# Two heads' scores as row tiles, two query tiles to a group, and a batch's scatters placed later in GpSimd's queue

## The chip, the cores and the metric

The kernel runs on one core of a Trainium2 chip. The metric is device microseconds (us) of one execution; less is better. PE is TensorE, DVE is VectorE, ACT is ScalarE, POOL is GpSimd, and SP is the engine whose queue issues the plain DMAs.

## The reference

Three stages run one after the other: causal windowed attention with a few global keys, then a mixture of experts in which each token goes to its best expert, then a second one with a fixed capacity for each expert.

```python
batch, n_heads, seq, head_dim = (4, 8, 768, 64)
n_global, n_local = (8, 96)
...
scores = scale * np.matmul(q, k.transpose(0, 1, 3, 2))
...
scores = scores + bias[None, :, :, :]
scores = np.where(keep, scores, -1000000000.0)
scores = scores - np.max(scores, axis=-1, keepdims=True)
a = np.exp(scores)
a = a / (np.sum(a, axis=-1, keepdims=True) + 1e-09)
return np.matmul(a, v).astype(np.float32)
...
x = np.ascontiguousarray(attn_out.transpose(0, 2, 1, 3)).reshape(B * S, H * D)
x = _moe_ref(x=x, **moe_kwargs)
return _moe2_ref(x=x, **moe2_kwargs)
```

The change lies in the attention stage and in the hand-over of its rows to the first experts, whose inputs are 3072 tokens of 512 numbers.

## The kernel before

The 4 batches and 8 heads make 16 pairs of heads, of which each is one step n = 4 b + hp of a loop. A head has 64 dimensions, so a pair's transposed queries and keys fill the 128 partitions. The 768 queries are six query tiles of 128. For query tile 0 a score tile has 128 columns (its own keys); for the others it has 232: 8 global keys, 96 before the tile and its own 128.

One step consists of these parts, by the lines of the profile:

- `prep` of the pair after this one: 12 transposes on PE (L402) bring keys (`kn`) and queries (`qn`) into PSUM tiles `tp`. DVE copies the keys into `kx` (L411, L414). ACT copies the queries into `qd` (L406), head 0 into partitions 0 to 63 of its first half, head 1 into partitions 64 to 127 of its second half; the other partitions of both halves were set to zero once. So a score matmul contracts over all 128 partitions, and the zeros cancel the other head's keys. POOL makes `va` and the global columns of `kx` by three copies (L417, L418, L420).
- `pair`: for each query tile two score matmuls on PE, one for each head (L444, into a PSUM tile `sc`, of which there are two, one bank each); DVE adds the bias and takes the minimum (L456); ACT takes the exponential (L458). PE transposes the probabilities into `pt` (L470), ACT copies them (`pts`, L472), and PE multiplies them with `vn` and `va` into `up` (L482), head 0 in output columns 0 to 63 and head 1 in 64 to 127 of the array.
- The results `ut` are copied out by DVE (L485), transposed on PE (L500) and scaled into the row tile `xr` (L501). After a batch's fourth pair `route` works out each token's place, and six indirect DMAs on POOL (L86, 128 rows each) scatter `xr` to `xs`. Experts read `xs` later: early loads `xa` of expert 0's first 240 rows (L604, on SP) are transposed on PE at L151 while attention is still running.

Every float32 matmul on two operands is recorded as two MATMULs with a LDWEIGHTS each. The order of an engine's instructions is made by a scheduler when the kernel is built; only SP's queue stands as written. PE, ACT, DVE and POOL each work through theirs in order, and an instruction that waits holds back all behind it. After attention, PE's order is written out by hand and is the same in both kernels. Scatters of batches 0 to 2 are issued from the loop by

```python
if n >= 6:
    while rows:
        rows.pop(0)()
```

Of the kernel before, what the change touches and what calls it, by code (L numbers as in the profile page):

```python
# [21 lines left out]
ROW = 516  # L22
# [7 lines left out]
def attention_moe_moe_kernel(  # L30
# [127 lines left out]
    def layer1(wa, xt, n, hs, cut=False, tags=("hp",)):  # L158

        xh, xl = xt  # L160
        for f in range(KF):
            if len(hs) == f:
                hs.append((m2.tile([128, SL], F32R, name=f"hh{f}"), m2.tile([128, SL], F32R, name=f"hl{f}")))
            hh, hl = hs[f]
            c = slice(f * 128, (f + 1) * 128)
            m = n // 2 if cut and f == 0 else n
            t_ = tags[f % len(tags)]
            for c0 in range(0, n, m):
                t = slice(c0, c0 + m)
                hp_ = pool_of[t_].tile([128, 512], F32, name="hp", tag=t_, bufs=1 if t_ == "gp" else None)  # L170
# [85 lines left out]
    with ExitStack() as actx:  # L256
# [114 lines left out]
        qds = []  # L371
        for i in range(2):
            qd = ac.tile([128, 2, S], F32, name=f"qd{i}")
            nc.gpsimd.memset(qd[0:64, 1], 0.0)
            nc.gpsimd.memset(qd[64:128, 0], 0.0)
            qds.append(qd)
        z = qds[0][64:128, 0, 0:ROW]
# [9 lines left out]

        def prep(b, hp, loads, first=False):
            qn, kn, vn = loads
            va = None  # L390
            qd = qds[hp % 2]
# [4 lines left out]
            if True:  # L396
                for (src, is_q), (g0, g1) in order:
# [6 lines left out]
                    if is_q:  # L404
                        for h in range(2):
                            nc.scalar.activation(qd[64 * h:64 * h + 64, h, c0:c0 + n],  # L406
                                                 tp[64 * h:64 * h + 64, :n], AF.Copy, scale=-0.125)
                    else:
                        t0, t1 = c0 // 128, (c0 + n) // 128
                        tpv = tp[:, :n].rearrange("p (t j) -> p t j", j=128)  # L410
                        nc.vector.tensor_copy(kx[:, t0:t1, k0:], tpv)  # L411
                        if not dense:
                            t2 = min(t1 + 1, NT)
                            nc.vector.tensor_copy(kx[:, t0 + 1:t2, 32:128], tpv[:, :t2 - t0 - 1, 32:128])  # L414
            if not dense:
                va = a2.tile([128, NT - 1, 2, D], F32, name="va")
                nc.gpsimd.tensor_copy(va, vn[:, :NT - 1])  # L417
                nc.gpsimd.tensor_copy(va[0:32], vgs[hp % 2][:, None].to_broadcast([32, NT - 1, 2, D]))  # L418
                if n_global:
                    nc.gpsimd.tensor_copy(kx[:, 1:, G0:32],  # L420
                                          kx[:, 0:1, 128:160 - G0].to_broadcast([128, NT - 1, 32 - G0]))
            return qd, kx, vn, va

        def pair(b, hp, ready, ut, sums, tiles=range(NT)):
            qd, kx, vn, va = ready
            upb = {}
            for t in tiles:
                if dense:
                    cols = [(0, 512), (512, S - 512)]
                    W, off, HW = S, 0, 1024  # L430
                elif t == 0:
                    W, off, HW = 128, 128, 256
                else:
                    W, off, HW = 256, G0, 256
                sc = ps.tile([128, 2, HW], F32, name="sc")
                p = a3.tile([128, 2, W], F32, name="p", tag="p") if dense else pbufs[t % 3]
                for h in range(2):
                    lhs = qd[:, h, 128 * t:128 * t + 128]
                    if dense:
                        for c0, n in cols:  # L440
                            nc.tensor.matmul(sc[:, h, c0:c0 + n], lhs,
                                             kx[:, c0 // 128:(c0 + n) // 128], start=True, stop=True)
                    else:
                        nc.tensor.matmul(sc[:, h, off:], lhs, kx[:, t, off:], start=True, stop=True)  # L444
# [60 lines left out]
        def route(b, ut, rec, xr, parts, tags=("tp", "tp")):  # L505
# [57 lines left out]
            return lambda: [scatter("xs", xs, si[:, t:t + 1], xr[:, T0 + t]) for t in range(nt)]  # L563
# [5 lines left out]
        batch, rows = {}, []  # L569
        todo = None  # L570
        for n in range(B * NP):
# [17 lines left out]
            if n >= 6:  # L589
                while rows:  # L590
                    rows.pop(0)()
# [17 lines left out]
            def todo(parts=(0, 3), tags=("tp", "tp"), steps="fn", b=b, hp=hp, ut=ut, uts=uts, sums=sums, rec=rec, xr=xr):  # L609
                if "f" in steps:  # L610
                    factors(hp, sums, rec, parts)
                    if hp == NP - 1:
                        rows.append(route(b, uts, rec, xr, parts, tags))
# [3 lines left out]
            if n < B * NP - 2:  # L617
                pair(b, hp, cur, ut, sums)
# [4 lines left out]
            else:  # L623
# [11 lines left out]
                rows.pop()()  # L635
# [11 lines left out]
        rows.pop()()  # L647

        counted = pick_order("tp")
        if EB:  # L650
# [12 lines left out]
            l1 = layer1(pre[0], xta, EA, hsa, tags=("sc",))  # L663
# [725 lines left out]
```

## Time and profile before

| | |
|---|---|
| median of 3 runs | 1009.27 us (1006.7 to 1011.89) |
| the profiled execution, its own time | 1016.74 us |
| its span in the trace, first to last instruction | 1015.0 us |
| PE busy | 951.0 us, 94% of the span |
| ACT busy | 425.0 us, 42% |
| DVE busy | 557.0 us, 55% |
| POOL busy | 298.5 us, 29% |
| granted TensorE clock, mean | 0.974 |

Attention fills about the first 250 us of the span. The shares are means over all stages. A busy PE counts the whole record of a matmul, from issue to a modelled end; records overlap, so the time that one more matmul costs is the distance between two starts, not the length of a record.

### The profile page before, as it was taken

Reading aid. Unit: us, or ns where it says so; the run is one execution under the profiler, and the core shown is the slowest. Engines: PE = TensorE matmul, PEld = TensorE weight load, DVE = VectorE, ACT = ScalarE, POOL = GpSimd, SP = SyncE. Lnnn points to the kernel's source line nnn. Section 1 sums busy time; section 2 is a strip of 40 time slices with the busy share of each in tenths; the row PEclk is TensorE's granted clock in tenths of the full one; section 3 lists DMA queues with packets and bytes.
Section 4 is the critical chain, followed back from the end, with each engine's and each line's share of the span. In section 5 each row is a group of like instructions: output and inputs, shape, how many; then the busy total and the mean of one; then the engine's idle time right before and its main releaser. Section 6 shows DMA issues by size and latency. Waiting matters only on the chain.

```text
span 1015.0 us, 17456 instructions
## 1 busy us (share of the span) xinstructions
PE 951.0 (94%) x6253; PEld 782.6 (77%) x6253; DVE 557.0 (55%) x1928; ACT 425.0 (42%) x939; POOL 298.5 (29%) x268
## 2 busy tenths in 40 slices
PE   8999889989996999999999979699999999999997
PEld 6877667767796999899897756487768677777996
DVE  6656566556332443423334344877878676785630
ACT  6886777856242433334224310133332323333531
POOL 3112333331235364464514861301020211102011
PEclk9999999999997999999999999889999999999999
DMA  7999654630355346534342311515243351615510
GB/s 156 212 200 211 165 144 123 136 120 3 118 175 178 126 143 206 149 136 136 125 146 83 111 44 40 207 53 187 94 146 128 102 187 42 219 65 176 169 59 31
DMA packets 124192, 133.24 MB, mean 131 GB/s; under 512 B 83445, under 2 KB 83585, under 8 KB 124097
## 3 DMA queue, kind: packets, MB, share of 16 engines
q1 hardware_dynamic: 114449, 105.96, 37.1%
q0 software_dynamic: 9648, 26.09, 7.8%
q8 instruction: 51, 0.84, 0.4%
q14 instruction: 44, 0.36, 0.1%
HBM read 103.77 MB, written 28.23 MB: 130 GB/s over the span
## 4 chain that ended last, share of the span: by engine, by line
PE 50%; issue 7%; DVE 7%; DMA 4%; POOL 2%; ACT 2%; POOLq 0%; SPq 0%; ACTq 0%; DVEq 0%
PE hp L175 22%; PE yp L207 13%; PE yp L191 7%; DMA raw<-in_moe_w_dram 3%; DVE wal L121 2%; PE hp L151 2%; ACT wah L119 1%; PE ip L1273 1%; POOL lg_dram L86 1%; PE cg L1125 1%; DVE wbl L121 1%; DVE geT L1114 1%; PE cp L1132 1%; PE hp L826 1%; PE hp L912 1%
## 5 line engine op out<-in xcount | busy, mean ns | idle before, releaser
L179 ACT ACTIVATE hh<-hp 128x384 fp32r<-128x384 f32 (+9 forms) x130 | 63.4, 491 | 200.3 <-PE hp L175 180.5
L180 DVE SCALAR_TENSOR_TENSOR hl<-hp,hh 128x384 fp32r<-128x384 f32 (+9 forms) x130 | 71.8, 555 | 117.9 <-ACT hh L179 113.6
L86 POOL DMA_INDIRECT out_dram<-yo,idx x24 | 25.8, 1074 | 265.6 <-ACT yo L1351 236.2
L458 ACT ACTIVATE pb<-pb,mn 128x232 f32<-128x232 f32 (+1 forms) x192 | 88.9, 465 | 18.6 <-DVE mn L456 18.1
L121 POOL TENSOR_TENSOR wbl<-raw,wbh 128x1024 fp32r<-128x1024 f32 x28 | 66.3, 2386 | 95.5 <-ACT wbh L119 55.5
L207 PE MATMUL yp<-wah,hh 128*128 128x512 f32 x224 | 93.0, 415 | 0.0
L444 PE MATMUL sc<-kx,qd 128*128 128x232 f32 (+1 forms) x384 | 90.4, 360 | 1.7 <-ACT qd L406 1.1
L207 PE MATMUL yp<-wah,hl 128*128 128x512 f32 x224 | 91.7, 410 | 0.0
L175 PE MATMUL hp<-xl,wah 128*128 128x240 f32 (+8 forms) x260 | 91.6, 352 | 0.0
L121 DVE TENSOR_TENSOR wal<-raw,wah 128x512 fp32r<-128x512 f32 (+1 forms) x78 | 67.4, 904 | 44.1 <-ACT wah L119 43.4
L175 PE MATMUL hp<-xh,wah 128*128 128x240 f32 (+8 forms) x260 | 90.7, 349 | 0.8 <-DVEq L835 0.6
L207 PE MATMUL yp<-wal,hh 128*128 128x512 f32 x224 | 91.0, 406 | 0.0
L119 ACT ACTIVATE wbh<-raw 128x1024 fp32r<-128x1024 f32 x60 | 62.3, 1057 | 68.2 <-DMA raw<-in_moe_w_dram 64.7
L175 PE MATMUL hp<-xh,wal 128*128 128x240 f32 (+8 forms) x260 | 90.5, 348 | 0.0
L175 PE MATMUL hp<-xh,wbh 128*128 128x384 f32 (+1 forms) x260 | 90.3, 347 | 0.0
L175 PE MATMUL hp<-xh,wbl 128*128 128x384 f32 (+1 forms) x260 | 89.9, 346 | 0.0
L175 PE MATMUL hp<-xl,wbh 128*128 128x384 f32 (+1 forms) x260 | 89.7, 345 | 0.0
L119 ACT ACTIVATE wah<-raw 128x1024 fp32r<-128x1024 f32 x68 | 68.5, 1052 | 43.1 <-DMA raw<-in_moe_w_dram 41.3
L456 DVE CUSTOM_DVE_ANT_0 pb<-sc,bias_w 128x232 f32<-128x232 f32 x160 | 56.9, 394 | 34.2 <-PE sc L444 18.0
L444 PEld LDWEIGHTS sc<-kx,qd 128*128 128x128 f32 x384 | 65.8, 199 | 9.6 <-issue 3.0
L121 POOL TENSOR_TENSOR wal<-raw,wah 128x1024 fp32r<-128x1024 f32 x22 | 58.2, 2657 | 43.2 <-ACT wah L119 26.6
L191 PE MATMUL yp<-hh,wbh 128*128 128x240 f32 (+5 forms) x192 | 65.2, 340 | 2.3 <-ACT yt L197 2.0
(303 smaller groups left out, 2145.4 us busy)
## 6 DMA issues: line engine op xcount, KB each, us to landing
raw<-in_moe_w_dram SPq DMA_DIRECT2D x128, 512.0 KB
xs_dram<-qd SPq DMA_DIRECT2D x8, 1032.0 KB
vn<-in_v_dram SPq DMA_DIRECT2D x32, 192.0 KB
kn<-in_k_dram SPq DMA_DIRECT2D x30, 192.0 KB
qn<-in_q_dram SPq DMA_DIRECT2D x30, 192.0 KB
rawg<-in_moe_w_dram SPq DMA_DIRECT2D x8, 512.0 KB
XB<-xs_dram SPq DMA_DIRECT2D x9, 241.9 KB
XB<-xs_dram SPq DMA_DIRECT2D x7, 258.0 KB
```

The costliest lines, as they stand in the source:

```text
L86: st = nc.gpsimd.indirect_dma_start(out=dst, out_offset=bass.IndirectOffsetOnAxis(ap=idx, axis=0), in_=src, in_offset=None)
L119: nc.scalar.activation(hi, raw, AF.Copy)
L121: lo_engine.tensor_tensor(lo[:, c], raw[:, c], hi[:, c], op=OP.subtract)
L151: tr = nc.tensor.transpose(tp[:, kk], rows[:, kk * 128:(kk + 1) * 128], ident[0:nt, 0:nt])
L175: nc.tensor.matmul(hp_[:, :m], a[:, c], b_[:, kk, t], start=(i == 0), stop=(i == 3 * KD - 1))
L179: nc.scalar.activation(hh[:, t], hp_[:, :m], AF.Relu)
L180: nc.vector.scalar_tensor_tensor(hl[:, t], hp_[:, :m], 0.0, hh[:, t], op0=OP.max, op1=OP.subtract)
L191: nc.tensor.matmul(yp, a[:, c], b_[:, :n], start=(f == 0 and i == 0), stop=(f == KF - 1 and i == 2))
L207: last_mm[0] = nc.tensor.matmul(yp, a[:, c], b_, start=(f == 0 and i == 0), stop=(f == KF - 1 and i == 2))
L444: nc.tensor.matmul(sc[:, h, off:], lhs, kx[:, t, off:], start=True, stop=True)
L456: nc.vector.tensor_tensor_reduce(p[:, h, off:], sc[:, h, off:], bt, 1.0, 3.0e38, OP.add, OP.min, mn)
L458: nc.scalar.activation(p[:, h, off:], p[:, h, off:], AF.Exp, bias=mn, scale=-1.0, accum_out=sums[:, t, hh:hh + 1])
```

## The change

It does these things:

- `qd` is one tile of 128 partitions (two buffers) without zero halves, filled by one ACT copy where there were two.
- A score matmul contracts over the 64 partitions of its head. Head 0 uses array rows 0 to 63 and head 1 rows 64 to 127; in the built program these matmuls have a tile size of 64 x 128, at row 0 and row 64.
- The scores of two query tiles are issued as one group of four matmuls into one PSUM tile of two banks, bank 0 for head 0 and bank 1 for head 1. There is one such tile, where there were two of one bank each.
- The scatters of a batch are held back by one step and are placed, one for each query tile, behind that tile's transposes, and behind POOL's copies for the next pair. This settles their place in the queue; they wait for nothing more at run time. For the last batch they stay where they were.
- The zeros that are written to `xs` come from a tile of their own.

```diff
-        z = qds[0][64:128, 0, 0:ROW]
+        z = ac.tile([64, ROW], F32, name="z")
+        nc.gpsimd.memset(z, 0.0)
...
+        last_copies = []
+
         def prep(b, hp, loads, first=False):
...
-            qd = qds[hp % 2]
+            qd = a2.tile([128, S], F32, name="qd")
...
                     if is_q:
-                        for h in range(2):
-                            nc.scalar.activation(qd[64 * h:64 * h + 64, h, c0:c0 + n],
-                                                 tp[64 * h:64 * h + 64, :n], AF.Copy, scale=-0.125)
+                        nc.scalar.activation(qd[:, c0:c0 + n], tp[:, :n], AF.Copy, scale=-0.125)
...
-                    else:
-                        nc.tensor.matmul(sc[:, h, off:], lhs, kx[:, t, off:], start=True, stop=True)
+                    W, off = (128, 128) if t == 0 else (256, G0)
+                    if i_ % 2 == 0:
+                        sc2 = ps.tile([128, 2, 2, 256], F32, name="sc", bufs=1)
+                        for k_, u in enumerate(tiles[i_:i_ + 2]):
+                            o = 128 if u == 0 else G0
+                            for h in range(2):
+                                hs_ = slice(64 * h, 64 * h + 64)
+                                nc.tensor.matmul(sc2[:, h, k_, o:], qd[hs_, 128 * u:128 * u + 128], kx[hs_, u, o:],
+                                                 start=True, stop=True)
+                    sc = sc2[:, :, i_ % 2]
+                    p = pbufs[t % 3]
...
-                            nc.tensor.transpose(pt[:, c, h], p[:, h, p0 + (c0 + c) * 128:p0 + (c0 + c + 1) * 128], ident)
+                            tr = nc.tensor.transpose(pt[:, c, h], p[:, h, p0 + (c0 + c) * 128:p0 + (c0 + c + 1) * 128], ident)
+                    if put:
+                        with tc.issue_after(tr.ins):
+                            put.pop(0)()
...
-            return lambda: [scatter("xs", xs, si[:, t:t + 1], xr[:, T0 + t]) for t in range(nt)]
+
+            def put(t):
+
+                st = scatter("xs", xs, si[:, t:t + 1], xr[:, T0 + t])
+                for c in last_copies:
+                    tc.add_manual_dep(st.ins, c.ins.name, mybir.DependencyInfo(
+                        mybir.DependencyClass.NoSync, mybir.DependencyReason.DATA), reason="order on GpSimd")
...
-            if n >= 6:
-                while rows:
-                    rows.pop(0)()
+            put = []
+            if 6 <= n < B * NP - 2:
+                put, late, rows = late, rows, []
...
-                pair(b, hp, cur, ut, sums)
+                pair(b, hp, cur, ut, sums, put=put)
+                for f in put:
+                    f()
```

How the built programs stand, at three places. The first is PE's queue in the middle of batch 0's fourth pair, from the scores of the pair's third query tile on (before: `sc_853`; after: `sc_813`). Before:

```order
L444 MATMUL sc_853<-kx_573,qd1_173 128x232 x2
L482 MATMUL up_685<-pts_731,va_422 64x128 x2
L482 MATMUL up_685<-pts_731,vn_388 64x128 x2
L470 MATMUL pt_821<-ident_71,pb1_166 128x128 x4
L444 MATMUL sc_874<-kx_573,qd1_173 128x232 x2
L500 MATMUL tp_784<-ident_71,ut_617 128x128 x3
L470 MATMUL pt_841<-ident_71,pb2_168 128x128 x4
L444 MATMUL sc_894<-kx_573,qd1_173 128x232 x2
```

PE's queue at the same place after the change (L445 is the score matmul, L474 the transposes, L489 the product with v, L507 the transposes of `ut`):

```order
L445 MATMUL sc_813<-kx_561,qd_560 128x232 x4
L489 MATMUL up_669<-pts_714,va_412 64x128 x2
L489 MATMUL up_669<-pts_714,vn_379 64x128 x2
L474 MATMUL pt_789<-ident_71,pb0_164 128x128
L507 MATMUL tp_766<-ident_71,ut_603 128x128 x3
L474 MATMUL pt_802<-ident_71,pb1_166 128x128 x4
L474 MATMUL pt_824<-ident_71,pb2_168 128x128
L507 MATMUL tp_771<-ident_71,ut_603 128x128 x3
L489 MATMUL up_788<-pts_792,vn_551 64x128 x2
L474 MATMUL pt_824<-ident_71,pb2_168 128x128 x3
L445 MATMUL sc_854<-kx_561,qd_560 128x232 x4
```

Two score matmuls for each tile became four for every two tiles, and they now stand next to full-array transposes with another tile size.

The second is POOL's queue around the scatters of batch 1. Before:

```order
L417 COPY va_1986<-vn_1952 128x640
L86 DMA xs_dram_66<-xr_917,si_1796 24576x516 x3
L418 COPY va_1986<-vg0_119 32x640
L86 DMA xs_dram_66<-xr_917,si_1796 24576x516 x3
L420 COPY kx_1961<-kx_1961 128x5x8
L121 TENSOR_TENSOR wal3_2309<-raw_2306,wah3_2308 128x1024
```

POOL's queue there after the change (L412, L413 and L415 are the three copies):

```order
L412 COPY va_1938<-vn_1905 128x640
L413 COPY va_1938<-vg0_119 32x640
L415 COPY kx_1915<-kx_1915 128x5x8
L86 DMA xs_dram_66<-xr_896,si_1758 24576x516 x6
L121 TENSOR_TENSOR wal3_2260<-raw_2257,wah3_2259 128x1024
```

The six scatters moved behind all three copies for pair 10, and still follow each other.

The third is POOL's queue around the scatters of batch 2, where the last two pairs of the loop are prepared. Before:

```order
L417 COPY va_2788<-vn_2754 128x640
L418 COPY va_2788<-vg0_119 32x640
L86 DMA xs_dram_66<-xr_1699,si_2592 24576x516 x6
L420 COPY kx_2763<-kx_2763 128x5x8
L417 COPY va_2969<-vn_2935 128x640
L418 COPY va_2969<-vg1_121 32x640
L420 COPY kx_2944<-kx_2944 128x5x8
```

POOL's queue there after the change:

```order
L412 COPY va_2724<-vn_2691 128x640
L413 COPY va_2724<-vg0_119 32x640
L415 COPY kx_2701<-kx_2701 128x5x8
L86 DMA xs_dram_66<-xr_1662,si_2538 24576x516 x6
L412 COPY va_2907<-vn_2874 128x640
L415 COPY kx_2884<-kx_2884 128x5x8
L413 COPY va_2907<-vg1_121 32x640
```

They moved behind `kx` of pair 14 and now stand between it and the copies for pair 15.

## Rows read from the trace of the kernel before

**Rows 1.** The page, part 1: busy us, share of the span, instructions.
```profile
PE 951.0 (94%) x6253; PEld 782.6 (77%) x6253; DVE 557.0 (55%) x1928; ACT 425.0 (42%) x939; POOL 298.5 (29%) x268
```

**Rows 2.** Stretches of attention: start:end, length, busy us and instructions, clock, DMA share, GB/s.
```profile
20.00:80.00 60.00, 60.00 (x486) 46.89 (x486) 37.72 (x170) 49.40 (x158) 6.86 (x13) 1.00 1.01 202
80.00:120.00 40.00, 37.10 (x295) 29.38 (x294) 23.06 (x102) 28.04 (x86) 13.23 (x16) 0.96 0.86 190
120.00:160.00 40.00, 36.34 (x295) 26.76 (x294) 24.78 (x103) 27.82 (x84) 16.91 (x16) 0.96 0.64 161
160.00:200.00 40.00, 40.00 (x310) 31.01 (x309) 24.72 (x113) 34.85 (x106) 9.91 (x11) 1.00 0.54 122
200.00:240.00 40.00, 36.02 (x282) 27.42 (x281) 24.75 (x119) 27.49 (x88) 12.73 (x14) 0.96 0.24 77
```

**Rows 3.** Groups by line, 0 to 400 us: busy, mean ns, idle before.
```profile
L444 PE MATMUL sc<-kx,qd 128*128 128x232 f32 x320 | 78.9, 371 | 1.0 <-DVE mn L456 0.6 <-ACT qd L406 0.3
L444 PE MATMUL sc<-kx,qd 128*128 128x128 f32 x64 | 13.0, 306 | 0.8 <-ACT qd L406 0.8
L444 PEld LDWEIGHTS sc<-kx,qd 128*128 128x128 f32 x384 | 65.8, 199 | 9.6 <-issue 3.0 <-DVE mn L456 2.7 <-ACT qd L406 2.0
L456 DVE CUSTOM_DVE_ANT_0 pb<-sc,bias_w 128x232 f32<-128x232 f32 x160 | 56.9, 394 | 34.2 <-PE sc L444 18.0 <-PE pt L470 8.8 <-ACT pb L458 5.6
L406 ACT ACTIVATE qd<-tp 64x256 f32<-64x256 f32 (+1 forms) x64 | 30.8, 482 | 9.0 <-PE tp L402 8.3
```

**Rows 4.** Timeline of PE, 228 to 252 us: start, length of the run, records.
```profile
232.55 0.95 PE L444 MATMUL sc<-kx,qd 128*128 128x232 f32 x4
233.33 0.49 PE L470 MATMUL pt<-ident,pb 128*128 128x128 f32 x3
...
237.51 0.39 PE L482 MATMUL up<-pts,vn 128*64 128x128 f32 x4
237.83 0.66 PE L470 MATMUL pt<-ident,pb 128*128 128x128 f32 x4
238.32 0.95 PE L444 MATMUL sc<-kx,qd 128*128 128x232 f32 x4
239.20 0.44 PE L482 MATMUL up<-pts,va 128*64 128x128 f32 x4
...
239.79 1.09 PE L470 MATMUL pt<-ident,pb 128*128 128x128 f32 x8
...
242.63 0.39 PE L482 MATMUL up<-pts,vn 128*64 128x128 f32 x4
242.84 0.39 PE L482 MATMUL up<-pts,va 128*64 128x128 f32 x4
```

**Rows 5.** Timeline of all engines in batch 1's scatters; in brackets idle time, releaser.
```profile
149.31 0.72 POOL L418 COPY va<-vg 32x640 f32<-32x640 f32 x1
150.20 0.99 POOL L86 DMA_INDIRECT xs_dram<-xr,si  x1 [0.17 <-issue]
151.49 0.96 POOL L86 DMA_INDIRECT xs_dram<-xr,si  x1 [0.30 <-issue]
152.32 0.56 DVE L485 COPY ut<-up 128x384 f32<-128x384 f32 x1 [3.78 <-remote]
152.44 0.60 ACT L472 ACTIVATE pts<-pt 128x512 f32<-128x512 f32 x1 [1.81 <-remote]
152.94 0.44 PE L482 MATMUL up<-pts,va 128*64 128x128 f32 x4 [2.49 <-issue]
```

**Rows 6.** Timeline: batch 2's first and last scatter, xa's loads, their first use.
```profile
207.97 1.01 POOL L86 DMA_INDIRECT xs_dram<-xr,si  x1 [2.21 <-DVE xr L558]
...
214.36 0.96 POOL L86 DMA_INDIRECT xs_dram<-xr,si  x1 [0.30 <-issue]
...
217.70 1.65 SPq L604 DMA_DIRECT2D xa<-xs_dram  x2
...
229.08 0.57 PE L151 MATMUL hp<-ident,xa 120*128 120x120 f32 x4
```

More of the change, by code (lines that the diff above doesn't have):

```diff
@@ L422, in prep, with pair @@
+                last_copies[:] = copies
             return qd, kx, vn, va
-        def pair(b, hp, ready, ut, sums, tiles=range(NT)):
+        def pair(b, hp, ready, ut, sums, tiles=range(NT), put=()):
             qd, kx, vn, va = ready
             upb = {}
-            for t in tiles:
+            tiles = list(tiles)
+            for i_, t in enumerate(tiles):
                 if dense:
                     cols = [(0, 512), (512, S - 512)]
-                    W, off, HW = S, 0, 1024
-                elif t == 0:
-                    W, off, HW = 128, 128, 256
-                else:
[L434 to L442, printed above, removed]
-                    else:
-                        nc.tensor.matmul(sc[:, h, off:], lhs, kx[:, t, off:], start=True, stop=True)
@@ new lines, in pair @@
+                    W, off = S, 0
+                    sc = ps.tile([128, 2, 1024], F32, name="sc")
+                    p = a3.tile([128, 2, W], F32, name="p", tag="p")
+                    for h in range(2):
+                        hs_ = slice(64 * h, 64 * h + 64)
+                        for c0, n in cols:
+                            nc.tensor.matmul(sc[:, h, c0:c0 + n], qd[hs_, 128 * t:128 * t + 128],
+                                             kx[hs_, c0 // 128:(c0 + n) // 128], start=True, stop=True)
+                else:
+                    W, off = (128, 128) if t == 0 else (256, G0)
[3 more added lines that the diff above has]
+                            o = 128 if u == 0 else G0
+                            for h in range(2):
+                                hs_ = slice(64 * h, 64 * h + 64)
+                                nc.tensor.matmul(sc2[:, h, k_, o:], qd[hs_, 128 * u:128 * u + 128], kx[hs_, u, o:],
+                                                 start=True, stop=True)
+                    sc = sc2[:, :, i_ % 2]
+                    p = pbufs[t % 3]
@@ L562, in route @@
             nc.vector.tensor_add(cum, cum, cs)
-            return lambda: [scatter("xs", xs, si[:, t:t + 1], xr[:, T0 + t]) for t in range(nt)]
+            def put(t):
[3 more added lines that the diff above has]
+                        mybir.DependencyClass.NoSync, mybir.DependencyReason.DATA), reason="order on GpSimd")
+            return [lambda t=t: put(t) for t in range(nt)]
         last_tr = [None]
@@ L568, in attention_moe_moe_kernel @@
             biases(range(2, H))
-        batch, rows = {}, []
+        batch, rows, late = {}, [], []
         todo = None
@@ L612, in todo @@
                     if hp == NP - 1:
-                        rows.append(route(b, uts, rec, xr, parts, tags))
+                        rows.extend(route(b, uts, rec, xr, parts, tags))
                 if "n" in steps:
@@ L634, in attention_moe_moe_kernel @@
                 todo2((0,), steps="n")
-                rows.pop()()
+                while rows:
+                    rows.pop(0)()
                 pair(*pair2)
@@ L646, in attention_moe_moe_kernel @@
         todo2((3,), steps="n")
-        rows.pop()()
+        while rows:
+            rows.pop(0)()
         counted = pick_order("tp")
```

18 lines of the change are left out of this document (6 added, 12 removed).

## The prediction

> **What bounds the kernel now.** I read the page's first part for the mean, then the stretches of attention, since only they are changed, then single starts on PE, and last the stretches where PE stands still. PE is busy 94% of the span, no other engine over 55% [rows 1]. In attention it is busier: 60.00 of 60 us and 40.00 of 40 in two of the five stretches, at a granted clock of 1.00; the other three miss 2.90, 3.66 and 3.98 us and show a clock of 0.96 [rows 2]. So PE's own work sets attention's length, and there are three disturbed places. ACT comes next, with 49.40 of 60 and 34.85 of 40 us [rows 2], that is 82 and 87%. The DMA engines are full (1.01) from 20 to 80 us, but PE missed nothing there.
>
> The kernel's other stages keep their instructions, and PE's order there is the same. They start when attention hands over, so I pass on to the end what attention gains, one for one.
>
> **What the matmuls cost.** A record's length (371 ns for a score matmul of 232 columns [rows 3]) is not its price, since records overlap. Four score records start at 232.55 and the next work at 233.33 [rows 4]: 0.195 us each. Full-array transposes of 128 columns cost (1.09 - 0.66) / 4 = 0.108 us each [rows 4]. With 320 records of 232 columns and 64 of 128 [rows 3] the scores cost 320 x 0.195 + 64 x 0.108 = 69.3 us of PE.
>
> Do two tiles of the array work side by side? Row tiles don't occur in this trace; the nearest row is the product with v, whose two heads write two halves of the array's columns. Four of its records, of 128 columns each, take 242.84 - 242.63 = 0.21 us [rows 4], where four full-array ones need 0.43: the two heads run at once, weight loads included. I take the same for two row tiles, whose two heads write different banks. Ends of the range: a full two as here, and no overlap at all. If all pairs met, 34.7 us would be left. In the built order the scheduler has torn 8 groups of four (one matmul and three, or such), which leaves a matmul without its partner: 8 x 2 x 0.195 = 3.1 us more, so 37.8. **Scores: -31.5 us.**
>
> A change of tile size costs time. From the product with v to transposes it is 237.83 - 237.51 = 0.32 us, where the next start of the same size came after 0.21; from scores to the product it is 239.20 - 238.32 = 0.88, where scores to transposes took 0.78 [rows 4]. That is 0.10 us for a change. Up to attention's last transposes, PE's order has 182 such changes before and 302 now, since scores stood among full-array work without a change and now need one on either side. **Changes of size: 120 x 0.10 = +12.0 us.** The new order also separates partners elsewhere: three pairs in the product with v (0.22 each), and the gate matmuls stand in three more runs (two records of 384 columns each, 0.65 by the 0.108 for 128). **+2.7 us.** PE's work falls by 16.8 us.
>
> The Trainium skill, page "TensorE: Matmul & The Clock Gate", section "Measured speedup vs the span model", gives 3.07 times for four row tiles of 32 rows and 512 columns, 77% of four. The column tiles in this trace reach the full two, and no run here shows a row tile yet. By 77%, as an estimate, the scores would need 49 us instead of 38, and the whole sum would come to nothing.
>
> **What waits more.** `sc` had two buffers of one query tile and has one buffer of two. The next group can start only when DVE has read all four halves of the last one. Behind it in PE's queue stand the product and transposes of tiles that are ready. The cover is the work between two groups, the 0.21 to 1 us pieces of rows 4; PE's wait for DVE at the scores was 0.6 us in total before [rows 3]. There are 48 groups. At the least they cost nothing; at the most I give each half a DVE read of 0.394 us [rows 3], 9.5 us. I take 2.5, near the low end, because the order has other work between groups. ACT gains: its `qd` copies handle both heads at once, half of 30.8 us [rows 3]. That is off the path, but it keeps ACT's load at about 85% when pairs get shorter, so I charge no wait for ACT. POOL loses four zero fills at the start, hidden by the first loads. The loads of pairs 1 to 5 run on full DMA queues [rows 2] and must come about 1 us a pair sooner. I charge nothing, since PE never missed one; with that cover gone it is at most 5 us.
>
> **The scatters.** All three stretches with idle time hold six scatters in a row, of 1.28 us each ((214.36 - 207.97) / 5 [rows 6]). What is late there? Batch 1's place shows it: DVE, ACT and PE all stand still for 2 to 4 us and go on within 0.6 us of each other, at 152.32, 152.44 and 152.94 [rows 5]. POOL's copy had ended at 150.03 and scatters ran on after it [rows 5]; no POOL copy releases them. So the queue behind the scatters is not what stops PE; something goes wrong while scatters are in flight. The change moves the scatters behind the copies and leaves six in a row, as POOL's order shows. I therefore take 0. The bounds: all goes, 10.5 us idle and 4% of clock in 3 x 40 us, -15.3; or each costs as much as the worst, about +2.
>
> The third burst gets a new neighbour. It now stands behind `kx` of pair 14 and in front of pair 15's copies, and `xa` can be loaded only when all its rows have landed. Before, the burst began at 207.97, `xa` was issued at 217.70 and used at 229.08 [rows 6]. Now, counted from the last key transpose of pair 14: POOL's copy at about +2, six scatters to +9.8; SP's issue came 2.4 us after the last scatter's end before (217.70 - 215.32 [rows 6]), so +12.2; for 495 KB I estimate 3 to 6 us, by the 77 GB/s of that stretch [rows 2] and twice that, so +15 to +18. PE's work up to the first `xa` transpose, by the prices above, is 11.6 us. Everything behind it in PE's queue waits too. PE may also wait at pair 15's scores, which need the copy behind the burst (+10.8 against +10.3), which takes part of the same wait. The bounds are 0 (PE is late anyhow by the burst itself) and 6; I take +3.5.
>
> **Sum:** -16.8 + 2.5 + 3.5 = -10.8 us. The profiled execution took 1016.74 us, its span 1015.0; the sum gives 1005.9 on it. That execution lies 7.5 us over the median of 1009.27, from which -10.8 gives 998.
>
> **Rivals.**
> - *The stalls at the scatters go as well.* For it: copies and scatters share one queue, and three stretches improve. Against it: rows 5. 998 - 15 = 983 us.
> - *Waits take the gain.* If each of the 48 groups costs 0.23 us more than I charge, or the early loads come late, the 10.8 us are gone: 1009 us. For it: one buffer for two tiles; against it: PE's 0.6 us of such waits so far.
> - *Row tiles meet only in part.* A score matmul's weight load takes 0.199 us [rows 3], no shorter than a step of 0.195; if the second head's load lags, a step of two heads takes 0.25 us, the scores 49 us, and the gain is zero: 1009 us. Against it: loads of the two column halves start together. The skill's 77% above would give this.
> - *Row tiles don't meet at all* (the slower side). The scores stay at 69.3, and changes of size (+12.0), torn partners (+2.7) and waits (+6.0) remain: +20.7, 1030 us. It decides from a step of two heads over 0.25 us; above that the change loses. For it: no row tile in this trace. Against it: the product with v.
>
> **How the numbers follow.** I give the forecast 0.60, the scatters' gain 0.10, the waits 0.12, part overlap 0.09 and no overlap 0.09. The forecast's own range, from its small terms, is 991 to 1005. To hold 8 in 10 I reach down to 985, which takes part of the first rival, and up to 1011 for the two that end at no change; no overlap stays outside. About 0.5% (5 us) is what a measurement of this kernel can tell from no change, so "faster" means below 1004: nearly all of the forecast and the first rival, 0.69. The two middle rivals and the forecast's upper end give 0.19 for the same; the rest, 0.12, is slower.
>
> **What would show it.** Score runs of eight records in about 0.8 us with a tile size of 64 x 128 (right), or about 1.6 us (wrong). PE's idle time at the scatters: still 2 to 4 us each. A wait of PE at L151's successor for `xa`. A PE that waits for DVE at the scores in every group would make me wrong, as would an ACT near 95% in attention.

## The result, and the profile after

The change made the kernel slower: 1020.24 us (median of 4 runs, 1018.32 to 1027.23) against 1009.93 (4 runs, 1006.7 to 1011.89), a ratio of 1.013 [1.0105, 1.0155]. The profiled execution took 1021.06 us, its span 1019.3. The prediction, 998 us, had the wrong sign.

The page of after, part 1, answers to [rows 1]; PE's work is smaller, as is ACT's and POOL's:

```profile
PE 946.9 (93%) x6253; PEld 755.9 (74%) x6253; DVE 556.7 (55%) x1928; ACT 406.2 (40%) x907; POOL 295.8 (29%) x265
```

The same stretches of attention as in [rows 2], after:

```profile
20.00:80.00 60.00, 57.59 (x479) 38.62 (x481) 35.43 (x158) 41.67 (x142) 6.58 (x12) 0.97 1.00 200
80.00:120.00 40.00, 36.53 (x321) 26.13 (x316) 27.43 (x116) 27.80 (x93) 10.47 (x14) 0.96 0.78 159
120.00:160.00 40.00, 35.94 (x281) 22.48 (x279) 21.01 (x96) 24.89 (x74) 17.20 (x18) 0.91 0.68 173
160.00:200.00 40.00, 38.78 (x301) 26.06 (x302) 24.66 (x111) 29.83 (x98) 11.18 (x12) 0.91 0.51 124
200.00:240.00 40.00, 37.03 (x291) 23.53 (x288) 27.89 (x120) 26.08 (x83) 13.75 (x14) 0.96 0.33 95
```

Two stretches in which PE was never idle, 20 to 80 and 160 to 200, now miss 2.41 and 1.22 us, and no stretch has a full clock. The saving on PE is there and is lost in waits. PE's longest waits after, 10 to 290 us (us in total, times, longest):

```profile
PE hp L175 <- DMA x_dram<-ya,ea_i: 4.9, 1, 4.9
PE gp L520 <- DVE ut L492: 3.5, 2, 2.8
PE pt L474 <- ACT pts L479: 3.5, 1, 3.5
PE pp L546 <- DVE oh L544: 2.9, 2, 2.2
PE tp L399 <- DMA kn<-in_k_dram: 2.4, 1, 2.4
PE tp L399 <- DVE xr L508: 1.7, 1, 1.7
```

Before, the waits at `hp` L175 and at `pts` were 0.6 and 0.3 us, and there was none for `kn`. The timeline of PE after shows a group of scores, to be held against [rows 4]:

```profile
177.88 0.44 PE L474 MATMUL pt<-ident,pb 128*128 128x128 f32 x2
178.25 1.05 PE L445 MATMUL sc<-kx,qd 64*128 64x232 f32 x8
179.23 0.44 PE L489 MATMUL up<-pts,va 128*64 128x128 f32 x4
```

Eight records take 0.98 us from their start to the next work's, where eight full-array ones needed 8 x 0.195 = 1.56. In the timeline of after the runs of four take 0.59 to 0.60. So a record costs (0.98 - 0.59) / 4 = 0.098 us, half of 0.195: the two heads run at once. On top comes a fixed 0.20 us for each run, not the 0.10 that I had charged for leaving a tile size. By single records, the steps of this run from pair to pair and to the next work are 0.30, 0.20, 0.20 and 0.29 us, so half of the fixed part lies behind the first pair and half behind the last. Entering costs 0.10 as charged: in after's one such place, four transposes ahead of scores take 0.59 us, before 0.49. The Trainium skill, page "TensorE: Matmul & The Clock Gate", section "Measured speedup vs the span model", gives 77% of the full factor for four row tiles; with the fixed part a run of eight here reaches 1.56 / 0.98 = 1.6, 80% of two, so the page's figure is near, though the trace puts the loss at the two ends of a run, not in the overlap.

### The profile page after: what moved, and what is told of

The parts are those of the page before. It is cut to its first block, busy times and chain, and to the rows that moved or that the text cites. A ratio compares the mean times of both kernels' runs of the same rounds, so it can differ in the third digit from the quotient of the medians.

```text
span 1019.3 us, 17384 instructions
## 1 busy us (share of the span) xinstructions
PE 946.9 (93%) x6253; PEld 755.9 (74%) x6253; DVE 556.7 (55%) x1928; ACT 406.2 (40%) x907; POOL 295.8 (29%) x265
## 4 chain that ended last, share of the span: by engine, by line
PE 64%; issue 10%; DVE 9%; DMA 8%; POOL 4%; ACT 2%; SPq 2%; another core or an unknown queue 0%; POOLq 0%; DVEq 0%; ACTq 0%
PE hp L175 21%; PE yp L207 13%; PE yp L191 7%; DMA raw<-in_moe_w_dram 4%; PE up L489 4%; PE pt L474 3%; PE sc L445 3%; DVE wal L121 2%; PE hp L151 2%; PE tp L399 2%; PE gp L520 2%; DMA kn<-in_k_dram 1%; POOL lg_dram L86 1%; PE ip L1292 1%; POOL wbl L121 1%
## 5 line engine op out<-in xcount | busy, mean ns | idle before, releaser
L175 PE MATMUL hp<-xh,wah 128*128 128x240 f32 (+8 forms) x260 | 90.8, 349 | 4.9 <-DMA x_dram<-ya,ea_i 4.9
L207 PE MATMUL yp<-wah,hh 128*128 128x512 f32 x224 | 93.2, 416 | 0.0
L175 PE MATMUL hp<-xl,wah 128*128 128x240 f32 (+8 forms) x260 | 91.7, 353 | 0.0
L207 PE MATMUL yp<-wah,hl 128*128 128x512 f32 x224 | 91.7, 409 | 0.0
L207 PE MATMUL yp<-wal,hh 128*128 128x512 f32 x224 | 91.1, 407 | 0.0
L175 PE MATMUL hp<-xh,wal 128*128 128x240 f32 (+8 forms) x260 | 90.7, 349 | 0.0
L175 PE MATMUL hp<-xh,wbh 128*128 128x384 f32 (+1 forms) x260 | 90.6, 348 | 0.0
L119 ACT ACTIVATE wbh<-raw 128x1024 fp32r<-128x1024 f32 x60 | 62.5, 1057 | 70.5 <-DMA raw<-in_moe_w_dram 67.5
L175 PE MATMUL hp<-xh,wbl 128*128 128x384 f32 (+1 forms) x260 | 90.1, 346 | 0.0
L175 PE MATMUL hp<-xl,wbh 128*128 128x384 f32 (+1 forms) x260 | 89.9, 346 | 0.0
L119 ACT ACTIVATE wah<-raw 128x1024 fp32r<-128x1024 f32 x68 | 68.4, 1052 | 45.5 <-DMA raw<-in_moe_w_dram 42.2
L474 PE MATMUL pt<-ident,pb 128*128 128x128 f32 x352 | 68.6, 301 | 5.3 <-ACT pts L479 3.5
L479 ACT ACTIVATE pts<-pt 128x512 f32<-128x512 f32 (+1 forms) x96 | 52.6, 553 | 37.2 <-PE pt L474 33.6
```

The costliest lines, as they stand in the source:

```text
L119: nc.scalar.activation(hi, raw, AF.Copy)
L207: last_mm[0] = nc.tensor.matmul(yp, a[:, c], b_, start=(f == 0 and i == 0), stop=(f == KF - 1 and i == 2))
L474: tr = nc.tensor.transpose(pt[:, c, h], p[:, h, p0 + (c0 + c) * 128:p0 + (c0 + c + 1) * 128], ident)
L479: nc.scalar.activation(pts[:, :n], pt[:, :n], AF.Copy)
```

## The experiments

Eighteen runs on four chips. Each ratio is against before on the same chip, whose median is 1001 to 1002 us on two of them and 1009 on the other two; where ratios of two chips are compared, that is said. 0.1% is 1 us. An edit can move more than it names, since the scheduler makes the order of PE, ACT, DVE and POOL anew for each kernel.

### Which part costs what

**e1_qd_back** is the whole change, but `qd` stays in the pool where it was:

```diff
-            qd = a2.tile([128, S], F32, name="qd")
+            qd = ac.tile([128, S], F32, name="qd", bufs=2)
```

> The whole change, with one word different: the two buffers of qd are taken from the pool in which the query halves lay before, so that the pool with the keys and rows starts above the end of the memory that xh and xl of the first experts take (in the changed kernel it starts below it). Theory of the boundary: xh and xl need not wait for the last early matmul, PE's 4.9 us of waiting in front of the first expert's matmuls are gone, and the second early scatter stands behind the overflow check again; 1014 to 1016 us. Rival, the late wait has another cause or is hidden elsewhere: 1020 us, and the wait stays.

**e2_row_tiles** is e1 with the scatters issued as before.

> Row tiles and groups of two query tiles alone, scatters issued as before, qd in the old pool. Theory that attention's waits eat the row tiles' gain wherever the scatters stand: 1010 to 1016 us, last product with v at 248 to 251 us. Rival, the moved scatters are what costs: 1000 to 1005 us, last product with v at 238 to 243 us.

**e3_scatter_move** is before with the scatters placed as in the change, and nothing else.

> The scatters' new place alone, scores and query halves as before. Theory that their place matters little: 1008 to 1012 us, still a stall of PE of 2 to 4 us at each burst. Rival, the moved scatters are what costs: 1015 to 1020 us.

**e4_low_bound** is before with one line changed, which moves the two `qd` to the pool `a2` and so the start of the memory behind attention's constants:

```diff
-            qd = ac.tile([128, 2, S], F32, name=f"qd{i}")
+            qd = a2.tile([128, 2, S], F32, name=f"qd{i}", bufs=1)
```

> The kernel before, with only its two query halves taken from the pool of keys and rows, so that this pool starts below the end of xh and xl, as in the changed kernel; nothing else is different. Theory of the boundary: the wait in front of the first expert's matmuls appears here too, 4 to 6 us over the kernel before, 1013 to 1016 us. Rival: no change, 1010 us.

Measured on one chip: e1 1.0130 [1.011, 1.015], e2 1.0059 [1.0043, 1.0075], e3 0.9979 [0.9963, 0.9995], e4 1.0057 [1.0035, 1.0079]. So the scatters' place is worth -2.1 us in the old kernel and +7.1 with row tiles (e1 against e2). The row tiles with their buffer cost 5.9 instead of giving 14.3. And a tile's pool alone costs 6.0 us (by the medians).

**b0_before** is the kernel before, profiled on that chip.

> The kernel before, unchanged, for a profile on the chip of these runs. Every theory expects the time of the kernel before. If the stalls of PE at the scatters belong to the kernel, they are here as in its first profile; if they belong to the one execution, they are gone.

**b1_after** is after, timed on another chip.

> The changed kernel, unchanged, on the chip of the other runs. If the pool boundary costs what the fourth experiment gave (6 us), it is 4 to 8 us above the first experiment, 1020 to 1024 us here, with a wait of about 5 us in front of the first expert's matmuls. Rival, the other late wait (3.5 us in the first experiment) covers the same time: 1015 to 1018 us.

Measured: b0 999.14 us; b1 1.0171 [1.0139, 1.0203].

### The pool of qd

`a2` lies behind `ac`. With `qd` gone from `ac`, `a2` begins at byte 132832 of a partition (before 143040), and the experts' pool that holds `xh` and, behind it, `xl` ends at 136736. So the end of that pool now lies over the start of `a2`, which early work uses until PE's last early matmul (L207). PE's timeline of after:

```profile
279.82 0.39 PE L207 MATMUL yp<-wbh,room 128*120 128x512 f32 x1
285.14 0.54 PE L175 MATMUL hp<-xh,wah 128*128 128x240 f32 x1 [4.93 <-DMA x_dram<-ya,ea_i]
```

ACT's timeline of after, same place:

```profile
280.29 1.03 ACT L154 ACTIVATE xh<-hp 128x480 fp32r<-128x480 f32 x2 [4.95 <-PE yp L207]
281.21 0.69 ACT L690 ACTIVATE ya<-yp,ea_s 120x512 f32<-120x512 f32 x1
```

ACT's copy into `xh`, the first write to that pool, waits for PE's L207; `ya` stands behind it, and PE then waits 4.93 us, which the trace puts down to the scatter of `ya`. The same place (hp L175) in the waits of e4, which has the shift alone, then b0, without it:

```profile
PE hp L175 <- DVEq L835: 6.2, 1, 6.2
```

```profile
PE hp L175 <- PEq L835: 0.4, 1, 0.4
```

5.8 us of the 6.0 lie there. In e1, with `qd` back, 3.5 us are left at this place. **e9_early_banks** looks for them: it is e2 with other PSUM banks for the first early layer.

```diff
-            l1 = layer1(pre[0], xta, EA, hsa, tags=("sc", "gp"))
+            l1 = layer1(pre[0], xta, EA, hsa, tags=("sc", "tp"))
```

> The second experiment (row tiles, scatters as before) with one word different: the early first layer takes turns between the PSUM buffers of sc and tp, not of sc and gp. gp's bank lies under the buffer that the transposes of the first expert's other rows (XB) need, so with gp they can't start before the early first layer's last copy-out. Theory: they come at least 3 us earlier against the end of the early work, the loads that follow them too, and the wait of 3.3 us in front of the first expert's matmuls goes: 1004 to 1006 us. Rival, the wait comes from elsewhere: 1009 us and the wait stays.

Measured 1.0045 [1.0026, 1.0064], on another chip than e2. The wait is gone, as the waits of e9 show:

```profile
PE hp L175 <- PEq L852: 0.5, 1, 0.5
```

So it came from the bank of `gp`, which the change put in place of a buffer of `sc`. That the time fell with it is not shown apart from the chip.

### The buffer of the scores

**e5_groups_only** is before with two query tiles to a group and one buffer of two banks, but matmuls on the full array. As in the change, the first early layer takes `gp`'s bank in place of a buffer of `sc`:

```diff
+                if i_ % 2 == 0:
+                    sc2 = ps.tile([128, 2, 2, 256], F32, name="sc", bufs=1)
+                    for k_, u in enumerate(tiles[i_:i_ + 2]):
...
+                            nc.tensor.matmul(sc2[:, h, k_, o:], qd[:, h, 128 * u:128 * u + 128], kx[:, u, o:],
```

> The kernel before, with its scores in groups of two query tiles and one buffer of two banks, but still as full-array matmuls; scatters and query halves as before. Theory that the single buffer costs by itself: 5 to 15 us over the kernel before, with PE waiting for DVE at the scores. Rival, one buffer costs nothing as long as PE has the full-array work to do: within 3 us.

**e8_groups_two_buffers** is e5, but each query tile of a group has a buffer of one bank of its own, and the early layer keeps to `sc`, as before:

```diff
-                    sc2 = ps.tile([128, 2, 2, 256], F32, name="sc", bufs=1)
+                    sc2 = []
...
+                        sc2.append(ps.tile([128, 2, 256], F32, name="sc"))
```

> As the fifth experiment (full-array scores of two query tiles issued together, all else as before), but each query tile has its own buffer of one bank, as before, and is released by itself. Theory of the single buffer (a group can start only when DVE has read all four halves of the last one): the cost of the fifth experiment goes, 999 to 1004 us. Rival, the order of issue in groups is what costs: 1015 to 1023 us.

Measured: e5 1.0226 [1.0204, 1.0249]; e8, on another chip, 0.9998 [0.998, 1.0016]. So it is not the grouping that costs, but the buffer, and to a smaller part the bank of `gp`. DVE's wait for scores, in total and times, in b0, in e5 and in e8:

```profile
  PE sc L444: 22.9, 25
```

```profile
  PE sc L442: 57.6, 35
```

```profile
  PE sc L443: 22.4, 25
```

The last product of attention starts at 235.9 us in b0 and 253.6 in e5, on the same chip; behind it, PE's wait at `hp` L175, the bank of `gp`, is 3.9 us in e5. In PE's list of waits hardly any of the 17.7 us stands under the scores. They are spread out, as one stretch of 210 us shows in b0 and in e5:

```profile
20.00:230.00 210.00, 207.62 (x1684) 160.25 (x1686) 136.63 (x610) 169.10 (x528) 59.07 (x68) 1.00 0.73 162
```

```profile
20.00:230.00 210.00, 202.60 (x1594) 153.77 (x1591) 128.21 (x570) 159.25 (x493) 56.83 (x67) 0.99 0.73 162
```

PE's idle time is only 5.0 us longer, yet PE has done 90 records (5%) less. A pause shorter than a record's length doesn't show as idle time, and a slow clock doesn't either. PE's timeline of e5, and the stretch with the eight scores:

```profile
143.36 0.44 PE L483 MATMUL up<-pts,va 128*64 128x128 f32 x4 [2.21 <-DVE ut L486]
...
144.71 3.33 PE L442 MATMUL sc<-kx,qd 128*128 128x232 f32 x8
147.97 0.57 PE L483 MATMUL up<-pts,va 128*64 128x128 f32 x4
```

```profile
144.70:148.00 3.30, 3.30 (x11) 2.43 (x10) 1.22 (x9) 0.92 (x6) 0.00 (x0) 0.53 0.00 0
```

Eight scores behind a pause of 2.21 us and 1.35 us of other work took 3.26 us, where most such runs in e5 take 1.57 to 1.67; the granted clock there is 0.53, about the lower level of 1.2 GHz. Over the 210 us the clock is 0.99 against 1.00 in b0, so this can be 2 us at most. The rest of the 17.7 us, behind the idle time and the clock, is in distances between records that all count as busy; no run takes it apart.

e2 is e5 with row tiles: 1.0226 to 1.0059, -16.7 us, and -13.5 at the last product (253.6 to 240.1).

Two kernels tried to give row tiles the missing buffer. Attention's PSUM tiles fill eight banks, before and after (two for `sc`, `tp` and `pt` each, one for `up` and `gp` each), and both kernels took theirs from other tiles.

**e10_three_banks**: head 0's scores with two buffers, head 1's with one, and `gp` and `tp` sharing.

> The ninth experiment with one PSUM bank more for the row tiles' scores: two buffers for head 0 and one for head 1, whose halves DVE reads first; gp's few tiles go to tp's buffers and up moves to the other pool. Theory of the single buffer: the next group of scores waits for two of DVE's four reads, attention ends 5 to 12 us earlier than in the ninth experiment, 993 to 1000 us, and the kernel is no slower than before. Rival, other waits (DMA, ACT behind the weights) hold it anyway: 1003 to 1007 us.

**e11_two_buffers**: e9 with two buffers of two banks; `tp` gets only one, and `gp` shares with `up`.

> The ninth experiment (row tiles, scatters as before) with two whole score buffers of two banks each; the banks come from tp, which keeps one buffer of two, and gp, which shares up's. Theory of the single buffer: DVE waits less for scores, attention ends 6 to 15 us earlier than in the ninth experiment, ratio to before 0.990 to 1.000. Rival, tp's single buffer or the loads hold PE up as much: ratio 1.002 to 1.015.

Measured: e10 1.0207 [1.0178, 1.0236]; e11 1.0228 [1.0194, 1.0262]. e10 answered nothing: in its order only about a quarter of the 96 pairs of heads still stood together (91 in e9), so it was hardly a row-tile kernel. In e11 PE waits at `tp` instead (for DVE's `xr` 4.9 us, `kx` 4.2, ACT's `qd` 4.1): the rival of its expectation.

Yet e11 shows what the second buffer is worth as long as nothing else stands in the way. The fifth pair's last product starts at 71.6 us in e11, at 82.3 in e9 and at 81.1 in b0. Part of that is order, for by then e11 has done 42 records less than e9; counted by records, PE's 560th starts at 73.9, 79.5 and 78.2 us. So e11 is 5.6 us ahead of e9 there. The loss comes in the pairs that hold a batch's scatters, the seventh, eleventh and fifteenth: each takes 31 to 38 us there and 18 to 21 in e9, with the transposes of the next pair and of the batch's rows taking turns at the single buffer of `tp`, and a granted clock of 0.67 to 0.77. In the first of the three PE's longest wait adds to it. POOL's and PE's timelines of e11:

```profile
93.62 1.14 POOL L86 DMA_INDIRECT xs_dram<-xr,si  x1 [8.33 <-DMA xs_dram<-z]
...
101.99 2.69 PE L445 MATMUL sc<-kx,qd 64*128 64x232 f32 x12 [5.86 <-POOL kx L415]
```

The first scatter waits until the last zeros for `xs` have landed, POOL's copy for the next pair stands behind the scatters, and PE's scores wait for that copy.

### ACT's queue

With the buffer known, +7.1 us for the scatters' place with row tiles were still open. Stretches behind the scatters of batch 0, of e1 and then of e2:

```profile
124.00:128.00 4.00, 0.68 (x9) 0.51 (x10) 0.00 (x0) 2.28 (x5) 1.47 (x3) 1.00 1.20 319
...
124.00:140.00 16.00, 12.68 (x80) 7.38 (x81) 4.76 (x22) 9.73 (x29) 4.11 (x5) 0.79 0.53 136
```

```profile
124.00:128.00 4.00, 4.00 (x35) 2.73 (x31) 0.57 (x3) 3.06 (x12) 1.16 (x1) 1.00 0.02 5
```

The timeline of e1 (POOL, SP, ACT):

```profile
116.61 1.15 POOL L86 DMA_INDIRECT xs_dram<-xr,si  x1 [0.18 <-issue]
...
117.82 0.35 SPq L116 DMA_DIRECT2D raw<-in_moe_w_dram  x1
...
120.16 0.19 ACT L462 ACTIVATION_READ_ACCUMULATOR pb<-pb,mn 128x1 f32 x1
...
123.14 0.96 POOL L86 DMA_INDIRECT xs_dram<-xr,si  x1 [0.30 <-issue]
...
125.72 1.06 ACT L119 ACTIVATE wah<-raw 128x1024 fp32r<-128x1024 f32 x1 [5.38 <-DMA raw<-in_moe_w_dram]
```

A chunk of the experts' weights (`raw`, 512 KB) is issued at 117.82 and is still under way at 125, with the scatters and the next pairs' loads on the same DMA engines (their share is 1.20). ACT's queue has the chunk's split (L119) at a fixed place, and ACT stands there for 5.38 us. All exponentials and `pts` copies behind it wait, and then PE, 3.32 of 4 us; the clock of the 16 us from 124 on is 0.79, another 3.4 us at most. Together that is 6.7, about the +7.1. ACT in e2 waits as long in total, but PE's longest wait for `pts` there is 0.5 us. After has such a stall too, but ahead of its scatters, which begin at 115.88: ACT waits for `raw` 3.77 us up to 105.91 (e1: 3.69 up to 106.62). So scatters are not the only traffic that can make a chunk late.

**e12_casts_later** is e1 with e9's banks, and the splits written one step later in the code; **e14_before_scatter_casts** is e3 with the same, **e13_both** is e11 with the same.

```diff
...
+            while held_back:
+                held_back.pop(0)()
+            hold[0] = n < B * NP - 1
...
```

> The whole change with qd in the old pool and the early layer on sc and tp (first and ninth experiment together), and the split of each early weight chunk (ACT's copy and POOL's subtraction) issued one step of the loop later than its load. Theory that ACT, standing at a chunk that has not landed, is what makes the moved scatters cost 7 us: ACT's waits for raw go, ratio to before 1.000 to 1.005. Rival, only the early layer's banks help: ratio 1.008 to 1.011.

> The eleventh experiment with the later splits of the twelfth (scatters as before). If both theories hold, the gains add: 2 to 6 us below the eleventh, ratio 0.985 to 0.997. If the splits don't matter without moved scatters, the same as the eleventh within 2 us.

> The kernel before with the scatters' new place (third experiment) and the later splits. If ACT's waits at the chunks matter while PE is full: ratio 0.994 to 0.997. If PE hides them: 0.997 to 1.000, as the third experiment.

Measured: e12 1.0131 [1.0099, 1.0163], e13 1.0227 [1.0194, 1.026], e14 1.0014 [0.9993, 1.0036]. The edit moved nothing: in e12 six splits stand behind exponentials 83, 96, 108, 120, 132 and 144 as without it, since the scheduler places them. All engines' orders are the same in e13 as in e11, and in e14 as in e3. So e14 repeats e3 on another chip, and the gain of 2.1 us from the scatters' place alone is not there (1.0014 against 0.9979). The waits of ACT in e12:

```profile
ACT wah L122 <- DMA raw<-in_moe_w_dram: 9.2, 4, 4.2
ACT wbh L122 <- DMA raw<-in_moe_w_dram: 3.0, 2, 2.4
```

**e15_casts_behind_exps** ties each split's place to the last exponential of the step after, so that the six stand behind 108, 120, 132, 144, 156 and 168; **e16_casts_old_scatters** is e15 with the scatters as before.

```diff
+            cast = nc.scalar.activation(hi, raw, AF.Copy)
+            if last_exp and hold[0]:
+                tc.add_manual_dep(cast.ins, last_exp[-1].ins.name, mybir.DependencyInfo(
+                    mybir.DependencyClass.NoSync, mybir.DependencyReason.DATA), reason="order on ScalarE")
```

> As the twelfth experiment, but the split of each of the first six weight chunks is ordered on ACT behind the last exponential of the next pair, two pairs (24 exponentials) later than before. Theory that ACT, standing at a chunk that has not landed, turns the moved scatters into a loss: ACT's waits for raw in attention (12 us in the twelfth) fall below 2 us, ratio to before 1.000 to 1.006 (1.013 in the first and the twelfth). Rival, PE waits elsewhere for the same time: 1.010 to 1.014.

> The ninth experiment (row tiles, scatters as before) with the splits of the fifteenth. The same theory: 2 to 6 us below the ninth, ratio to before 0.998 to 1.003. Rival: as the ninth, 1.0045.

Measured, on one chip: e15 0.9989 [0.9971, 1.0006], e16 1.0036 [1.0016, 1.0056]. In e15 ACT waits for no `raw` any more, and the stretches of e15 with the first two bursts are full, at full clock:

```profile
80.00:120.00 40.00, 39.89 (x355) 28.50 (x355) 28.12 (x128) 29.86 (x103) 11.17 (x16) 1.00 0.95 214
120.00:160.00 40.00, 40.00 (x350) 27.04 (x349) 29.15 (x134) 32.34 (x103) 17.69 (x18) 1.00 0.72 170
```

From e12 to e15 (two chips) the time falls by 1.4%, and by as much from e1, whose chip has the same time of before as e15's, though e1 also has the bank of `gp`. The edit names the order on ACT alone, but POOL's subtractions of the same chunks move with it, and parts of PE's and DVE's order are new as well. So the stall is shown as a cause by its place (in e1 PE stands while ACT waits; in e15 both waits are gone), and its size is not isolated. With the old place of the scatters the same edit gives far less: e9 1.0045, e16 1.0036, on two chips. And the scatters' place, +7.1 us with ACT's stall, is now worth -4.7 (e15 against e16). In e16 PE waits for the copy behind the scatters of batch 0, as in e2; the second line is POOL's first scatter in e2:

```profile
PE sc L456 <- POOL kx L426: 3.7, 1, 3.7
```

```profile
97.37 1.15 POOL L86 DMA_INDIRECT xs_dram<-xr,si  x1 [10.29 <-DMA xs_dram<-z]
```

As in e11, the scatters wait for the zeros to land, with the copy behind them in POOL's queue. Before has the same 10.10 us on POOL, but no wait of PE for that copy. In their new place the first scatter waits for nothing (0.18 us in e1), so 3.7 of the 4.7 us are likely this wait.

### The early loads

**e6_half_fill_before** is before, and **e7_half_fill_row_tiles** is e1, each without the zeros for the first 256 rows of each expert, which the tokens write over with these inputs. That takes DMA work out of the first 80 us.

```diff
-                    nc.sync.dma_start(xs[e * N:e * N + SL].rearrange("(j p) w -> p j w", p=SL // 8),
+                    nc.sync.dma_start(xs[e * N + SL // 2:e * N + SL].rearrange("(j p) w -> p j w", p=SL // 16),
```

> The kernel before, without the zero fill of the first 256 rows of each expert, which tokens overwrite with these inputs: half of the fill's 8.3 MB is left out. Theory that the DMA queues and PE are even in the first 93 us: 0 to 4 us faster than the kernel before, since PE is busy nearly all of that time anyway. Rival, the fills cost nothing at all: no change.

> The whole change with qd in the old pool (as in the first experiment), without the same half of the zero fill. Theory that full DMA queues set the first 100 us of the changed kernel, so that row tiles can't shorten it: the sixth pair's last product with v comes at 85 to 89 us (93 to 94 in all kernels so far), and the time is 6 to 12 us below the first experiment, ratio to before 1.000 to 1.007. Rival, the queues don't matter and PE waits for other engines there: the sixth pair still ends at 93 us, ratio 1.012 to 1.014.

Measured: e6 1.0015 [1.0, 1.0029], e7 1.0077 [1.0051, 1.0103], that is 5.3 us less than e1 and nothing in the kernel before. The stretch of e7 is full again where after and e1 waited for `kn`:

```profile
20.00:80.00 60.00, 60.00 (x519) 40.47 (x519) 38.83 (x181) 44.76 (x155) 7.99 (x14) 1.00 0.72 155
```

The sixth pair's last product starts at 89.1 us in e7 and at 94.2 in e1, so the fill costs row tiles 5 us up to there. Without row tiles it costs nothing: 93.5 in e6, 92.8 in b0. But the loads alone don't set that pace, as the expectation had it: with the full fill the place is reached at 98.2 us in e5 and at 84.4 in e11, by their buffers (e11 has done 659 records by then, the others 692).

## Why the prediction was wrong

The sum was -10.8 us; measured were +10.3 at first and +17 on another chip.

- **Scores -31.5, changes of size +12.0, torn partners +2.7 (net -16.8): nearly right.** Full overlap is shown, the fixed cost of a run is 0.20 instead of 0.10 us. From start to next work, 376 of the 384 score records take 74.7 us in b0 and 52.9 in e15, 21.8 less where -31.5 and half of the 12.0 make 25.5; without idle time behind a run it is 24.0 less. So the net is up to 3.7 us smaller, -13 or a little more, as in -13.5 at the last product from e5 to e2. Neither rival on part overlap or none came.
- **One buffer +2.5 (0 to 9.5): the step that failed most.** e5 against e8 (two chips) gives about 2.3% with the bank of `gp` (3.9 us) in it, so 17 to 19 us on the full array; with row tiles only e11's first five pairs show it, 5.6 us ahead of e9 at an equal count of records. I took PE's own 0.6 us of waits at the scores as the measure, and "other work between groups" as cover. But the buffer also decides when DVE has something to do: its waits for scores rose from 22.9 to 57.6 us, and tiles come later through the whole chain. That the waits take the gain was a rival with 0.12, priced at no change; it came larger. Whether the loss comes from waits at run time or from the order that the scheduler chose for one buffer is not told apart.
- **"I charge no wait for ACT": failed.** I asked how busy ACT would be (41.67 of 60 us from 20 to 80, 69%, where I had said 85), not what stands in its queue. A split that waits for its load stops the exponentials behind it, as e1 and e15 show.
- **The scatters 0, xa +3.5: wrong in place.** PE waited at most 1.8 us for `xa` (e15), and in after next to nothing. The scatters' place is worth -2.1 and +1.4 us in the old kernel (e3 and e14, two chips), gives 4.7 with row tiles where ACT doesn't stand (e15 against e16), and costs 7.1 where it does (e1 against e2). I had judged POOL's queue by batch 1 alone, where no copy releases PE. At batch 0 the first scatter waits 10 us for the zeros, and PE, once faster, 3.7 us for the copy behind the scatters. What I took 0 for, the stalls during scatters, stayed in after (`gp` 3.5, `tp` at `xr` 1.7), as forecast; the loads that the scatters meet were not in the sum.
- **"I pass on to the end what attention gains, one for one": failed.** The moved `qd` and the bank of `gp` made the first experts wait: 5.8 us in e4, 2.9 to 3.5 in e1 and e2, 4.9 in after. The order there is the same, as I said; the memory is not.
- **Early loads 0 (at most 5): the upper end was right.** e7 gives 5.3 us.

Of the two signs that I had named for being wrong, neither came: in after PE waits 0.6 us for DVE at the scores, and ACT is at 69%. The losses stand in DVE's waits and in ACT's queue.

One buffer with the bank +22.6 (e5), row tiles -16.7 (e2), scatters with ACT's stall +7.1 (e1) and the pool of `qd` +4.1 (b1, on another chip) make +17.1, which is b1's 1.0171. But these are the steps of one chain from before to b1, so they must add up, and that is no check of them. The only independent price is e4's 6.0 us for the pool, where the chain has 4.1. The first ratio, 1.0130 [1.0105, 1.0155], is smaller; the two intervals overlap.

No version is clearly faster than before. e15 repairs the three losses except the buffer and ends where before is; the scatters' place alone is 2 us faster on one chip and not on another.

## What to carry to other kernels

When an edit makes PE's work shorter, price a lost buffer by what the engine that reads it does meanwhile, not by the writer's waits in the old trace, which had the buffer. For each in-order queue look at what stands in it that can wait for a DMA, and ask which transfers the edit moves next to that DMA; a busy share of 69% says nothing about it. And where a tile changes its pool, compare the addresses and banks of what comes after, since an unchanged order can still wait.

## What the runs showed of the hardware

The same program before has a different profile on another chip. In b0 the stretches with scatter bursts are these (compare [rows 2]: 37.10, 36.34 and 36.02 of 40 us at a clock of 0.96):

```profile
80.00:120.00 40.00, 38.80 (x325) 30.91 (x324) 26.38 (x114) 29.50 (x89) 13.41 (x17) 1.00 0.92 207
120.00:160.00 40.00, 39.44 (x324) 30.15 (x323) 27.20 (x121) 32.65 (x104) 17.42 (x17) 1.00 0.72 174
...
200.00:240.00 40.00, 39.30 (x320) 28.80 (x317) 26.01 (x115) 27.11 (x82) 10.71 (x12) 1.00 0.20 67
```

PE is idle 2.5 us there instead of 10.5, and the span is 997.4 instead of 1015.0 us. So the stop of all engines in [rows 5], which I read as a cost of the scatters, belongs to the chip as much as to the kernel. e3 and e14, the same program on two chips, say so too: in the three stretches PE is busy 40.00, 40.00 and 39.10 us in e3, and 39.79, 35.00 and 37.52 in e14. Two of the four chips of the experiments have before at 1009 us and two at 1001 to 1002; e3's and b0's is one of the fast two, e14's one of the others. PE's wait at `gp` goes the same way: 3.5 us in after, 3.4 in b1 and 3.5 in e12, but 0.7 in e1 on the chip of b0. What it is, no run tells.
